# A linear-attention and gated-FFN kernel: lam moves to ScalarE's queue, and one activation table serves logarithm and exponential

## The chip, the cores and the metric

The kernel runs on one core of a Trainium2 chip. The metric is device time in microseconds (us) from one execution; lower is better. Three runs of the kernel before took 203.37, 203.39 and 203.57 us. The engines are TensorE (PE, with its weight loads PEld), VectorE (DVE), ScalarE (ACT), GpSimd (POOL) and SyncE (SP). SyncE computes nothing here; it issues transfers. GpSimd and ScalarE can issue transfers too, each on its own queue. The transfers of all queues run on the core's 16 DMA engines.

## The reference

Two parts follow each other. First a decayed linear attention over q, k and v of shape (4, 8, 768, 64), with one decay `lam` for each of 8 heads:

```
Dmask = where(rel >= 0, lam ** rel, 0)
for each block b of 64 positions:
    intra = ((qb @ kb.T) * Dmask) @ vb
    inter = (qb * lam ** (pos + 1)) @ kv_state
    out[b] = intra + inter
    kv_state = lam ** 64 * kv_state + (kb * lam ** (63 - pos)).T @ vb
```

Then, with x the attention output as 3072 tokens of 512 features:

```
h = x @ w_in        # 512 -> 2048
g = h * cos(h)
y = g @ w_out       # 2048 -> 512
```

## The kernel before

The 3072 tokens are 24 blocks of 128. The powers of lam are not computed by powers: a logarithm of lam is taken once (`lnl`), multiplied by positions (`expo_sp`, `expo`), and exponentials of that scale q, k and v ahead of the matmuls (`q_sp`, `k_sp`, `q_scale`, `v_scale`). These few small instructions on ScalarE and VectorE stand in lines 215 to 230. lam comes as a broadcast of 8 numbers to 128 partitions (4 KB, 32 bytes for each partition) by a transfer that SyncE issues in line 188. ScalarE reads its functions from tables. The build puts a table load ahead of an activation whose function isn't in the loaded set: one ahead of the logarithm (L216), one ahead of the first exponential (L221), and one ahead of a sine (L232), which is computed once on a dummy so that the table for the cosine of the FFN is there early.

The first four blocks are loaded as two "spans" of two blocks each, so that a transfer moves longer pieces: SyncE issues q, k of span 0 and then q, k of span 1 (called q0, k0, q1, k1 here; tile `sp_f`, L269, 512 KB each). GpSimd issues v of both spans (`v_sp`) and then the weights `w_in` and `w_out`, on its own queue; the first v load waits until q0 has landed. Each span load is scaled in two halves (L609): q0, k0 and q1 on VectorE, k1 on GpSimd, 1.29 us and 2.04 us for the pair of halves. TensorE transposes the halves (L617), ScalarE copies the transposes to SBUF (L620), TensorE multiplies scores (L628), VectorE masks them (L633), and TensorE makes the values (L641, L654, L660). From there on the hidden layer (L748, cosine on ScalarE L754, product on VectorE L760) and the projection (L794) fill TensorE, with the attention of later blocks worked in between.

The order on every engine is written by a planner: each piece of work is a task with an engine, a duration, what it depends on and a priority, and `Planner.order` simulates all engines and DMA and emits tasks in order of their planned start. `Planner.SETUP` gives the time at which each engine, and the DMA, is free for its first task. Where the plan leaves TensorE idle in the lead-in, `keep_awake` puts matmuls on a blank tile or on the identity into the gap (L882, L886), of a width that follows from the planned gap; their result is not used.

Of the kernel before, what the change touches and what calls it, by code (L numbers as in the profile page):

```python
# [56 lines left out]
class Planner:  # L57


    LAT = {"PE": 0.2, "ACT": 0.06, "DVE": 0.08, "POOL": 0.1, "SP": 0.0, "DMA": 0.0, "SETUP": 0.0}  # L60

    SETUP = {"POOL": 3.7, "DVE": 5.6, "ACT": 7.3, "SP": 1.3, "DMA": 2.9}

    def __init__(self, bufs):
        self.tasks, self.bufs = [], bufs
# [6 lines left out]
    def order(self):  # L72
        free, done = dict(self.SETUP), []
        got = {tag: [] for tag in self.bufs}
        owner = [None] * BANKS
        only = {}
        todo = list(self.tasks)
        while todo:
            first = {}
            for t in todo:  # L80
                if only.get(t.eng, t) is not t:
                    continue
                at = self.ready(t, got)
                if at is None:
                    continue
                if t.banks:
                    b = self.free_banks(t, owner)
                    if len(b) < t.banks:
                        continue
                    t.bank = b[:t.banks]  # L90
                    at = max([at] + [x for x, _ in t.bank])
                at = max(at, free.get(t.eng, 0.0))
                first.setdefault(t.eng, []).append((at, t))
            best = None
            for eng, c in first.items():
                t0 = min(a for a, _ in c)
                a, t = min(((a, t) for a, t in c if a <= t0 + 1e-6 + t.worth), key=lambda x: x[1].issue.end if eng == "DMA" else x[1].prio)
                if best is None or a < best[0]:
                    best = (a, t)
            assert best, "no task can start"  # L100
            a, t = best
            t.start, t.end = a, a + t.dur
            free[t.eng] = t.end
            only.pop(t.eng, None)
            if t.then:
                only[t.eng] = t.then
            if t.get:
                got[t.get].append(t)
            if t.banks:
                t.bank = [i for _, i in t.bank]  # L110
                for j, i in enumerate(t.bank):
                    owner[i] = (t, j)
            todo.remove(t)
            done.append(t)
        return sorted(done, key=lambda t: t.start)
# [29 lines left out]
def kernel(  # L145
# [10 lines left out]
    nc = tc.nc  # L156
    B, H, S, D = q.shape
    P = 128
# [26 lines left out]
        return psum.tile(shape, dt, tag=f"bank{i}", bufs=1, name=name)  # L185

    lam_bc = consts.tile([P, H], F32)
    nc.sync.dma_start(out=lam_bc, in_=bass.AP(tensor=lam.tensor, offset=lam.offset, ap=[[0, P], [1, H]]))
    pos = consts.tile([P, NB], F32)
    nc.gpsimd.iota(pos, pattern=[[P, NB]], base=-S // 2, channel_multiplier=1,  # L190
                   allow_small_or_imprecise_dtypes=True)
# [657 lines left out]

    idle = pl.add("SETUP", 0.0, [], None, -1e9, banks=1)  # L850
    for x in range(SPANS):
# [74 lines left out]
```

## Time and profile before

| | |
|---|---|
| median of three runs | 203.39 us |
| span of the profiled execution, first to last instruction | 201.6 us |
| TensorE busy | 193.4 us (96%) |
| ScalarE busy | 120.6 us (60%) |
| VectorE busy | 116.1 us (58%) |
| GpSimd busy | 64.5 us (32%) |

The times of the profile are counted from the first instruction. The profile gives one execution only, and its span leaves out what lies before the first and after the last instruction, 1.8 us against the median. "The chain that ended last" follows the last instruction back, at each step to what released it. An idle time is put down to whatever came last by the profile. "SPq" is SyncE's work of issuing a transfer, "issue" is time in which an engine waited for nothing that the profile shows. In the transfer views "q1" is the queue of SyncE, "q0" that of GpSimd, and "q10" that of ScalarE.

### The profile page before, as it was taken

How to read it: one execution, taken by the hardware profiler on the slowest of the kernel's cores; microseconds unless marked ns; L12 is line 12 of the kernel's file. 1: busy time of each engine (PE TensorE's matmuls, PEld its weight loads, DVE VectorE, ACT ScalarE, POOL GpSimd, SP SyncE). 2: the span in 40 equal slices, each digit the busy share in tenths (PEclk: the TensorE clock that was granted, in tenths of full speed). 3: DMA queues.
4: the chain of work that ended last, by engine and by line, in shares of the span. 5: the costliest groups of instructions: out<-in, count | busy, mean ns of one | idle time of the engine just before them, and what ended most of it. 6: DMA issues, size and time to landing. Idle time of an engine off the chain costs nothing.

```text
span 201.6 us, 5921 instructions
## 1 busy us (share of the span) xinstructions
PE 193.4 (96%) x2444; PEld 116.7 (58%) x2472; DVE 116.1 (58%) x229; ACT 120.6 (60%) x242; POOL 64.5 (32%) x85
## 2 busy tenths in 40 slices
PE   6899999999999999999999999999999999999994
PEld 2467544557757857767658676755445544444442
DVE  2779782267855958758458575834578454444001
ACT  5988870239738868566639666654877464345120
POOL 5694003076045172735455372525500000000000
PEclk9999999999999999999999999999999999999999
DMA  4999999999879999999999899969900010111112
GB/s 125 320 192 193 201 206 227 197 208 215 210 187 235 253 221 221 233 159 247 214 281 234 187 225 220 234 146 283 233 0 3 3 52 0 52 55 52 52 52 104
DMA packets 96762, 33.94 MB, mean 168 GB/s; under 512 B 84832, under 2 KB 93792, under 8 KB 96736
## 3 DMA queue, kind: packets, MB, share of 16 engines
q1 hardware_dynamic: 89232, 28.78, 62.5%
q0 software_dynamic: 7360, 4.72, 16.4%
q8 instruction: 19, 0.31, 0.7%
q10 hardware_dynamic: 144, 0.07, 0.1%
q14 instruction: 7, 0.06, 0.1%
HBM read 27.27 MB, written 6.29 MB: 166 GB/s over the span
## 4 chain that ended last, share of the span: by engine, by line
PE 92%; DMA 3%; issue 1%; SPq 1%; POOL 1%; ACT 0%; POOLq 0%; ACTq 0%
PE ps_h L748 42%; PE ps_f L794 41%; DMA sp_f<-in_k_dram 3%; PE ps_s L423 2%; PE ps_o L518 2%; PE ps_kv L435 1%; PE ps_o L486 1%; SPq L269 1%; PE ps_o L654 1%; PE ps_kv L641 1%; POOL k_sp L609 1%; PE ps_x L486 0%; PE ps_t L375 0%; PE ps_t L617 0%; PE ps_o L660 0%
## 5 line engine op out<-in xcount | busy, mean ns | idle before, releaser
L760 DVE TENSOR_TENSOR g<-ps_h,cos 128x256 bf16<-128x256 f32 (+1 forms) x149 | 73.0, 501 | 42.0 <-ACT cos L754 41.1
L754 ACT ACTIVATE cos<-ps_h,halfpi 128x256 f32<-128x256 f32 (+1 forms) x149 | 75.8, 536 | 29.3 <-PE ps_h L748 28.2
L748 PE MATMUL ps_h<-xT,w_in_sb 128*128 128x256 bf16 (+1 forms) x591 | 90.4, 303 | 0.4 <-issue 0.2
L794 PE MATMUL ps_f<-w_out_sb,g 128*128 128x512 bf16 (+2 forms) x377 | 87.6, 370 | 2.1 <-issue 1.4
L748 PEld LDWEIGHTS <-w_in_sb 128*128 128x128 bf16 x596 | 57.6, 98 | 29.9 <-DVE xT L526 0.4
L794 PEld LDWEIGHTS <-g 128*128 128x128 bf16 x400 | 37.6, 98 | 37.2
L345 POOL TENSOR_TENSOR qk<-q_f,q_scale 128x512 bf16<-128x512 f32 x19 | 19.6, 1044 | 35.0 <-DMA q_f<-in_q_dram 23.8
L808 ACT COPY o_sb<-ps_f 128x512 f32<-128x512 f32 (+1 forms) x24 | 13.7, 572 | 24.7 <-PE ps_f L794 23.4
L353 POOL TENSOR_TENSOR v_s<-v_f,v_scale 128x512 bf16<-128x512 f32 x19 | 19.7, 1042 | 11.5 <-DMA v_f<-in_v_dram 9.0
L428 DVE TENSOR_TENSOR s_m<-ps_s,mask 128x512 bf16<-128x512 f32 x20 | 13.0, 685 | 4.2 <-PE ps_s L423 3.7
L349 POOL CAST qk<-k_f 128x512 bf16<-128x512 f32 x18 | 11.0, 611 | 7.9 <-DMA k_f<-in_k_dram 7.9
L526 ACT CAST xT<-ps_o 128x512 bf16<-128x512 f32 x11 | 6.0, 588 | 9.0 <-PE ps_o L518 5.7
L441 DVE TENSOR_TENSOR sum<-sum,ps_kv 128x512 f32<-128x512 f32 x15 | 10.2, 682 | 0.6
L446 ACT CAST S<-sum 128x512 bf16<-128x512 f32 x15 | 9.2, 617 | 0.9 <-DVE sum L441 0.8
L269 POOL DMA_DIRECT2D w_out_sb<-in_moe_w_out_dram x4 | 3.0, 784 | 15.6 <-DMA q_f<-in_q_dram 15.6
L808 DVE COPY o_sb<-ps_f 128x384 f32<-128x384 f32 x1 | 0.6, 558 | 11.5 <-DMA out_dram<-o_sb 11.5
L886 PE MATMUL ps_idle<-blank 128*128 128x512 f32 (+2 forms) x8 | 5.0, 770 | 1.6 <-DVE blank L212 1.6
L486 PEld LDWEIGHTS <-v_s 64*64 64x64 bf16 x320 | 4.0, 107 | 4.2 <-issue 3.4
L503 DVE COPY spare<-ps_o 1x1 f32<-1x1 f32 x6 | 0.9, 156 | 8.4 <-PE ps_o L486 8.4
L633 DVE TENSOR_TENSOR s_m_sp<-ps_s,mask_sp 128x512 bf16<-128x512 f32 x8 | 5.1, 685 | 1.2 <-PE ps_s L628 1.2
L486 PE MATMUL ps_o<-s_m,v_s 64*64 64x64 bf16 x256 | 5.1, 196 | 0.0
L518 PE MATMUL ps_o<-qkT,S 64*64 64x64 bf16 x304 | 4.9, 195 | 0.0
(74 smaller groups left out, 90.9 us busy)
## 6 DMA issues: line engine op xcount, KB each, us to landing
q_f<-in_q_dram SPq DMA_DIRECT2D x20, 256.0 KB, 3.7
k_f<-in_k_dram SPq DMA_DIRECT2D x20, 256.0 KB, 4.3
v_f<-in_v_dram SPq DMA_DIRECT2D x20, 256.0 KB, 4.9
out_dram<-o_sb SPq DMA_DIRECT2D x19, 256.0 KB, 2.6
w_out_sb<-in_moe_w_out_dram POOLq DMA_DIRECT2D x4, 512.0 KB, 12.3
sp_f<-in_q_dram SPq DMA_DIRECT2D x2, 512.0 KB, 5.2
sp_f<-in_k_dram SPq DMA_DIRECT2D x2, 512.0 KB, 5.8
w_in_sb<-in_moe_w_in_dram POOLq DMA_DIRECT2D x2, 512.0 KB, 8.6
```

What stands on the lines that cost most here:

```text
L345: vec[e].tensor_mul(new_qk()[:, 0, :, s], live.pop(("q_f", 2 * pr + s)), q_scale[:, c, :].unsqueeze(2).to_broadcast([P, H, D]))
L349: (nc.scalar.copy if early else nc.gpsimd.tensor_copy)(new_qk()[:, 1, :, s], live.pop(("k_f", 2 * pr + s)))
L353: vec[e].tensor_mul(live["v_s", 2 * pr + s], live.pop(("v_f", 2 * pr + s)), v_scale[:, c, :].unsqueeze(2).to_broadcast([P, H, D]))
L428: nc.vector.tensor_mul(t, live["s", pr][s], mask.unsqueeze(1).to_broadcast([P, H, D]))
L441: nc.vector.tensor_add(new, live["sum", pr, 0] if half else live["sum", pr - 1, 1], live["kv", pr][half])
L446: nc.scalar.copy(new_S(pr, half), live["sum", pr, half])
L486: yield lambda h=h: nc.tensor.matmul(o[halves[h % 2], h // 2], lhsT=live["v_s", n0 + s][m, h, :], rhs=live["s_m", n0 + s][m, h, :], start= ...
L748: nc.tensor.matmul(t[:, :n], lhsT=w_in_sb[:, kd, f * P:(f + 1) * P], rhs=live["xT", i][:, kd, at], start=(kd == 0), stop=(kd == KD - 1))
L754: nc.scalar.activation(c[:, :n], live["h", i, f, at.start][:, :n], AF.Sin, bias=halfpi)
L760: return nc.vector.tensor_mul(live["g", i][:, f, at], live.pop(("h", i, f, at.start))[:, :n], live.pop(("c", i, f, at.start))[:, :n])
L794: nc.tensor.matmul(live["f", i, j, piece][:, :width], lhsT=live["g", i][:, f, j * P:(j + 1) * P], rhs=w_out_sb[:, f, part], start=(f == 0) ...
L808: (nc.scalar.copy if eng == "ACT" else nc.vector.tensor_copy)(o[:, :width], live["f", i, j, piece][:, :width])
```

## The change

lam's transfer is issued by ScalarE in place of SyncE, so that q0 is SyncE's first transfer. Right behind it ScalarE loads one table set that holds both the logarithm and the exponential, which leaves two table loads in the kernel: this one and the sine's. The planner's set-up times for VectorE, ScalarE, SyncE and the DMA are lowered. Line numbers behind the edit are one higher in the changed kernel.

```diff
-    SETUP = {"POOL": 3.7, "DVE": 5.6, "ACT": 7.3, "SP": 1.3, "DMA": 2.9}
+    SETUP = {"POOL": 3.7, "DVE": 4.95, "ACT": 6.0, "SP": 0.85, "DMA": 2.45}
...
     lam_bc = consts.tile([P, H], F32)
-    nc.sync.dma_start(out=lam_bc, in_=bass.AP(tensor=lam.tensor, offset=lam.offset, ap=[[0, P], [1, H]]))
+    nc.scalar.dma_start(out=lam_bc, in_=bass.AP(tensor=lam.tensor, offset=lam.offset, ap=[[0, P], [1, H]]))
+    nc.scalar.preload_act_table_set("natural_log_exp_and_others")
     pos = consts.tile([P, NB], F32)
```

The new set-up times leave the order of all planned work as it was, on every engine. Only the fillers on TensorE differ: the first run of `keep_awake` is 512 + 512 + 128 columns wide in place of 512 + 512 + 256, the filler on the identity behind the second half of k0's transposes is gone, and the one ahead of k1's transposes is 512 columns wide in place of 320.

## The prediction

> **What bounds the kernel now.** I read the chain that ended last first, by share and then its opening stretch in order of time, because the change touches only the first microseconds.
>
> ```profile
> PE 92%; DMA 3%; issue 1%; SPq 1%; POOL 1%; ACT 0%; POOLq 0%; ACTq 0%
> ...
> 0.81 0.40 SPq L188
> ...
> 1.26 0.42 SPq L269
> ...
> 1.73 0.58 SPq L269
> ...
> 2.35 1.49 SPq L269
> ...
> 3.89 6.28 DMA sp_f<-in_k_dram
> ...
> 10.34 1.05 POOL k_sp L609
> ...
> 11.44 0.40 PE ps_t L617 x4
> ```
>
> The columns are start, duration and what. TensorE bounds the kernel from 11.44 us on: 92% of the chain is its matmuls, and its pieces follow each other with gaps of 0.05 to 0.16 us to the end. Nothing in the diff touches that. Ahead of it lies a lead-in set by SyncE's queue: lam's issue at 0.81, then q0, k0, q1, k1 (the two span loads of q and of k), then k1's landing at 10.17 and its scaling on GpSimd. The kernel gets shorter by as much as k1 lands earlier, if what meets it at 11.44 is earlier too.
>
> Second, the timeline of the lead-in on the other engines, because the change also reorders ScalarE.
>
> ```profile
> 0.80 1.28 ACT L216 ACT_TABLE_LOAD   x1 [0.80 <-PEq L910]
> ...
> 3.70 0.21 ACT L216 ACTIVATE lnl<-lam_bc 128x8 f32<-128x8 f32 x1 [1.62 <-DMA lam_bc<-in_lam_dram]
> 3.93 1.28 ACT L221 ACT_TABLE_LOAD   x1
> 4.02 0.18 DVE L218 TENSOR_TENSOR expo_sp<-pos_sp,lnl 128x16 f32<-128x16 f32 x1 [1.98 <-ACT lnl L216]
> ...
> 5.22 0.22 ACT L221 ACTIVATE q_sp<-expo_sp 128x16 f32<-128x16 f32 x1
> ...
> 5.47 1.29 DVE L609 TENSOR_TENSOR q_sp<-sp_f,q_sp 128x512 bf16<-128x512 f32 x2 [1.03 <-ACT q_sp L221]
> 5.59 1.96 POOL L269 DMA_DIRECT2D v_sp<-in_v_dram  x2 [1.93 <-DMA sp_f<-in_q_dram]
> 5.81 1.28 ACT L232 ACT_TABLE_LOAD   x1
> ...
> 7.22 1.29 DVE L609 TENSOR_TENSOR k_sp<-sp_f,k_sp 128x512 bf16<-128x512 f32 x2 [0.46 <-DMA sp_f<-in_k_dram]
> ...
> 8.71 1.29 DVE L609 TENSOR_TENSOR q_sp<-sp_f,q_sp 128x512 bf16<-128x512 f32 x2 [0.20 <-DMA sp_f<-in_q_dram]
> ```
>
> The brackets give the idle time before and what ended it. VectorE's first scaling waits for the factors q_sp (5.44), but q0's landing is nearly as late: 5.26 by the transfer view, 4.0 us after its issue. The next two scalings wait for loads, k0 and q1, with VectorE idle before each. So the table load at 3.93 holds VectorE back by some 0.2 us, which the wait for k0 swallows, and the loads set the pace.
>
> Third, the DMA view of 1.6 to 3.6 us (rates in 40 slices of 0.05 us), and of 6.5 to 9.0 us.
>
> ```profile
> GB/s 0 0 0 0 3 3 3 4 4 3 3 4 3 4 14 95 65 1 2 34 34 63 52 64 31 42 42 33 86 75 145 75 94 156 227 246 256 276 328 317
> DMA packets 418, 0.14 MB, mean 72 GB/s; under 512 B 144, under 2 KB 418, under 8 KB 418
> ```
>
> ```profile
> q1 hardware_dynamic: 1714, 0.87, 114.8%
> ```
>
> From 1.8 to 2.3 us only lam's 32-byte pieces move (3 to 4 GB/s); the first burst of q0 comes at 2.35, 1.09 after q0's issue at 1.26, and the rate needs until about 3.5 to reach the 347 GB/s that the second window shows. In that second window every packet is of SyncE's queue, though v_sp was issued on GpSimd's at 5.59.
>
> **The change, step by step.** All sums are made against the profiled execution: span 201.6 us, which stands 1.8 below the median of 203.39; I keep the 1.8.
>
> 1. lam's issue leaves SyncE: 0.40 and the 0.05 gap behind it. q0 issues at 0.81 instead of 1.26, the other three follow. If data follow issues at the same distance, q0, k0, q1 and k1 land 0.45 earlier, k1 at 9.72. v_sp (issued when q0 lands) and all weight loads behind it on GpSimd's queue move with them: -0.45 on the path.
>
> 2. How far lam's pieces themselves hold up q0 is not separable here. Lower bound of the gain: 0, if the same pieces hold the same DMA engines from 1.8 until about 3.3 whichever queue brought them. Upper bound: the stream runs at full rate from 0.81 + 1.04 = 1.85 instead of about 3.3, that is -1.45. I take 0.45 because the rows show the first q0 burst 1.09 behind its own issue, as lam's first piece is 1.0 behind its own; that is nearest to a plain shift.
>
> 3. lam's issue goes to ScalarE, ahead of everything there. By SyncE's row it costs 0.40, by the last store's row on ScalarE's queue 0.37. The table load then runs from about 1.25 to 2.53, still before lam lands at 3.7 (ScalarE idled 1.62 there): cost 0, cover 1.1 us. Nothing else is queued behind it that could start earlier.
>
> 4. The table load at 3.93 goes (1.28). The factor q_sp then waits only for expo_sp: 4.20, so q_sp is ready by 4.5 and q0's landing (4.81) ends the wait. Of the 1.28 the path gets nothing beyond step 1; the load of q0 is late next. The last table load moves from 5.81 to about 4.85 and no longer holds the first transposed copy (7.22), which becomes 0.5 to 0.9 earlier; kT's copies, behind k0's landing, move by 0.45 only.
>    The row here says 1.28 and an ACTIVATE 0.01 after the load. The Trainium skill, ScalarE: Activation LUTs, What ACT_TABLE_LOAD costs, prices a switch at about 2.66 us, with a drain of 1.38 that this trace doesn't show; by it ScalarE would save 2.66. The sum is the same by both, because the load of q0 covers it.
>
> 5. TensorE's keep-awake matmuls follow the planner's shifted set-up times: the opening run loses 128 columns of 1280, one filler behind the k0 transposes goes, and the one ahead of k1's transposes grows from 320 to 512 columns. All real work keeps its order on every engine. The grown filler: 320 columns took 0.76 from 10.38; 192 more at four passes are 768 columns, 0.33 us at the rate of the projection's row in the chain (28 matmuls of 512 columns in 6.21 us, 2.3 columns per ns). It starts at 10.38 - 0.45 = 9.93 and ends at 11.02; k1's first half is ready from GpSimd at 11.39 - 0.45 = 10.94, and its transposes began 0.05 later. Cost 0 to 0.05; I take 0. If k1 gains more than 0.5, this filler is late next, though it too moves with q1.
>    The opening run took 4.25 for its 1280 columns at four passes (1.2 columns per ns, against the 2.3 above), so the shorter one ends near 5.4, and the first transposes come at about 5.77: a gap of 0.4, as now (5.80 to 6.22). The Trainium skill, TensorE: Matmul & The Clock Gate, Part 1, speaks against a shorter run: full speed comes after a busy window of 3.41 us whose phase is free. By that rule the run of 3.85 leaves 0.44 for the phase where 4.25 left 0.84. The sum without the rule is 0; by it a missed window costs up to another window at half speed, over a stretch that mostly waits for loads.
>
> 6. From 11.44 on TensorE's work is the same and its loads move with the stream: w_in and w_out are queued behind v_sp. 0.
>
> Sum: 203.39 - 0.45 = 202.94, span about 201.15.
>
> **Rivals.**
>
> *More is gained* (0.2): lam's pieces no longer stand ahead of q0 in its queue, and the slow ramp shrinks. For it: 144 packets under 512 B in the window and 3 to 4 GB/s until 2.3. Between 0.6 and the bound of 1.45; middle 0.9, 202.5. TensorE's and VectorE's lead-in would have to follow, so I doubt the whole.
>
> *Nothing* (0.15): the ramp belongs to the first accesses or to lam wherever it is issued, and k1 lands between 9.9 and 10.2. For it: the bursts at 2.35 are followed by 0.6 us at under 70 GB/s, which an earlier issue may not cure. 203.1 to 203.4.
>
> *Slower: lam is served late* (0.15). q0 and lam now start within 0.01 us on two queues. In 6.5 to 9.0 us the engines served one queue alone while another had work issued. If lam waits behind q0, k0 or more, the factors are late. From lam's landing to VectorE's scaling are 0.8 us (3.69 to 4.49 without the load). VectorE has three scalings of 1.29 ahead of the masking at 9.92, so it must start by 5.60 to keep step 1, and by 6.05 to lose nothing: lam may land at 4.8, or 5.25. Behind q0 alone (4.81) it costs nothing much; behind k0 too (7.13 - 0.45 = 6.68) VectorE starts at 7.5 and ends at 11.35, +1.4, 204.8; behind all four +4, 207. Against it: lam has only 4 KB and nothing ahead of it at 0.8 us, and the ScalarE queue's one store landed 1.6 us after its issue, not later than SyncE's.
>
> *Slower: the clock comes late* (0.05). If full speed came only after the stretch from 10 to 15 us, its 4.7 us of TensorE work would take up to as much again; likelier 0.3 to 1. From 203.5 up.
>
> **How the numbers follow.** The plain shift has 0.45, with a spread of 0.3 to 0.65 for steps 2 and 5; three quarters of it lie beyond 0.2% (0.41 us, about what a measurement of this kernel can tell from no change). Faster: 0.34 + 0.2 = 0.54, and 0.01 of the third case. Within 0.2%: 0.11 + 0.13 = 0.24. Slower: 0.15 + 0.05, and 0.01 of the third = 0.21. The likeliest case alone is 202.7 to 203.1. The range for 8 in 10 reaches into the larger gain, 202.2, and to the mild end of a late lam, 203.9; outside it lie half of the two slower cases and the end of the larger gain.
>
> **What would show it.** Step 1: q0's issue at 0.81, k1 landing at about 9.7, GpSimd's scaling at 9.9, first k1 transposes near 11.0. Step 2: the rate passes 300 GB/s at 3.0 for a plain shift, at 2.0 to 2.5 for the larger gain, at 3.5 for none. Step 4: two table loads instead of three, and the first VectorE scaling ended by q0's DMA. The late lam would show as VectorE or ScalarE waiting for lam beyond 4.8, the late clock as transposes of 0.40 us growing longer after 6 us. I am wrong if k1 lands earlier and TensorE's start at 11.44 doesn't move: then the filler, a mask or w_in would end that wait.

## The result, and the profile after

The changed kernel takes 204.62 us (median of 6 runs, 204.00 to 205.52) against 203.38 for the kernel before (6 runs, 203.17 to 203.57). The ratio is 1.0067, 95% interval 1.0052 to 1.0083: 0.67% slower. The forecast was 202.9 with a range of 202.2 to 203.9: the time was to fall by 0.45 us and rose by 1.24.

The profiled execution of the changed kernel took 204.37 us, with a span of 202.7, 1.1 longer than before. These are rows of its lead-in on the timeline, those of the transfers and of what waits for them; the rows between are left out (start, duration, engine, line, what, and in brackets the idle time before it and what ended that; "ACTq" is ScalarE's work of issuing a transfer):

```profile
0.80 0.43 ACTq L188 DMA_DIRECT2D lam_bc<-in_lam_dram  x1
0.81 0.46 SPq L270 DMA_DIRECT2D sp_f<-in_q_dram  x1
1.32 0.57 SPq L270 DMA_DIRECT2D sp_f<-in_k_dram  x1
1.93 2.56 SPq L270 DMA_DIRECT2D sp_f<-in_q_dram  x1
4.46 0.21 ACT L217 ACTIVATE lnl<-lam_bc 128x8 f32<-128x8 f32 x1 [1.92 <-DMA lam_bc<-in_lam_dram]
4.53 1.45 SPq L270 DMA_DIRECT2D sp_f<-in_k_dram  x1
...
6.02 1.29 DVE L610 TENSOR_TENSOR q_sp<-sp_f,q_sp 128x512 bf16<-128x512 f32 x2 [0.82 <-DMA sp_f<-in_q_dram]
7.56 1.29 DVE L610 TENSOR_TENSOR k_sp<-sp_f,k_sp 128x512 bf16<-128x512 f32 x2 [0.25 <-DMA sp_f<-in_k_dram]
9.02 1.29 DVE L610 TENSOR_TENSOR q_sp<-sp_f,q_sp 128x512 bf16<-128x512 f32 x2 [0.16 <-DMA sp_f<-in_q_dram]
10.65 2.04 POOL L610 TENSOR_TENSOR k_sp<-sp_f,k_sp 128x512 bf16<-128x512 f32 x2 [0.96 <-DMA sp_f<-in_k_dram]
11.75 0.40 PE L618 MATMUL ps_t<-ident,k_sp 128*128 128x128 bf16 x4
```

q0 is issued 0.45 earlier, as the diff says. But everything that waits for data is later: q0's scaling starts at 6.02 instead of 5.47, k1's at 10.65 instead of 10.34, and k1's transposes at 11.75 instead of 11.44. lam is later too (its logarithm at 4.46 instead of 3.70). All three VectorE scalings, and GpSimd's, wait for a load.

The DMA view of 1.6 to 3.6 us of the changed kernel (40 slices of 0.05 us) shows where q0 lost its lead:

```profile
GB/s 0 0 0 0 1 3 3 1 1 3 1 1 3 1 2 1 3 3 1 55 42 72 62 64 64 52 33 43 42 72 74 115 115 115 85 115 114 135 124 146
...
q1 hardware_dynamic: 166, 0.08, 17.4%
q10 hardware_dynamic: 110, 0.00, 2.5%
```

Until 2.5 us only lam's 32-byte pieces move, now on ScalarE's queue (q10). q0's first burst comes at 2.55, 1.75 after its issue, where it was 1.09 before. After that SyncE's queue (q1) stays under 150 GB/s until 3.8 us, with lam's pieces still on their way. At 3.6 us it has moved 0.08 MB, where the same window before moved 0.14. By the packets of the trace, lam's 128 pieces took from 1.82 to 3.33 before and from 1.84 to 4.10 after, and the rate passed 300 GB/s at 3.5 before and at 4.2 after. In both kernels full speed comes when the last piece of lam is through.

At k1's transposes the changed kernel is 0.31 us behind. The rest of the 1.1 comes later. TensorE's work stands 0.66 behind at 21 us and stays near that until 139, where it falls to 1.04 behind. The page's group of weight loads for `w_in`, first before and then after, and a row from TensorE's waits after, name the two places:

```profile
L748 PEld LDWEIGHTS <-w_in_sb 128*128 128x128 bf16 x596 | 57.6, 98 | 29.9 <-DVE xT L526 0.4
...
L749 PEld LDWEIGHTS <-w_in_sb 128*128 128x128 bf16 x596 | 57.3, 98 | 30.5 <-DMA w_in_sb<-in_moe_w_in_dram 0.7
```

```profile
PE ps_s L424 <- DMA qkT<-qk: 0.3, 1, 0.3
```

Before, the longest wait named for that group was for VectorE (0.4 us), and no matmul waited for a transposed copy `qkT`. These two places are those of one execution (204.37, when the six took 204.00 to 205.52); another can lose its time elsewhere. The chain that ended last, by share, now has 8% of DMA where it had 3%:

```profile
PE 88%; DMA 8%; ACT 1%; SPq 1%; DVE 0%; issue 0%; ACTq 0%; DVEq 0%
```

So the loads are late at the start, and nothing makes that good later: between 36 and 60 us the kernel before moves 4.91 MB, the changed one 4.76. The difference is about what a shift of 0.66 us makes at 205 GB/s, an estimated 0.14 MB.

### The profile page after: what moved, and what is told of

Read it like the earlier page. It is cut to its first block, busy times and chain, and to the rows that moved or that the text cites. A ratio compares the mean times of both kernels' runs of the same rounds, so it can differ in the third digit from the quotient of the medians.

```text
span 202.7 us, 5946 instructions
## 1 busy us (share of the span) xinstructions
PE 196.5 (97%) x2471; PEld 116.5 (57%) x2471; DVE 116.2 (57%) x229; ACT 119.7 (59%) x241; POOL 64.5 (32%) x85
## 4 chain that ended last, share of the span: by engine, by line
PE 88%; DMA 8%; ACT 1%; SPq 1%; DVE 0%; issue 0%; ACTq 0%; DVEq 0%
PE ps_h L749 40%; PE ps_f L795 38%; DMA v_f<-in_v_dram 3%; DMA sp_f<-in_k_dram 3%; DMA qkT<-qk 2%; PE ps_s L424 2%; PE ps_o L519 1%; PE ps_kv L436 1%; PE ps_o L487 1%; PE ps_t L618 1%; PE ps_s L629 1%; PE ps_o L655 1%; PE ps_kv L642 1%; PE ps_x L487 0%; PE ps_idle L887 0%; PE ps_t L376 0%
## 5 line engine op out<-in xcount | busy, mean ns | idle before, releaser
L749 PE MATMUL ps_h<-xT,w_in_sb 128*128 128x256 bf16 (+1 forms) x596 | 91.4, 303 | 0.0
L795 PE MATMUL ps_f<-w_out_sb,g 128*128 128x512 bf16 (+2 forms) x400 | 91.3, 371 | 0.0
L442 DVE TENSOR_TENSOR sum<-sum,ps_kv 128x512 f32<-128x512 f32 x15 | 10.2, 682 | 0.6
L887 PE MATMUL ps_idle<-blank 128*128 128x512 f32 (+1 forms) x8 | 5.3, 811 | 1.6 <-DVE blank L213 1.6
```

The source lines that it names most:

```text
L442: nc.vector.tensor_add(new, live["sum", pr, 0] if half else live["sum", pr - 1, 1], live["kv", pr][half])
L749: nc.tensor.matmul(t[:, :n], lhsT=w_in_sb[:, kd, f * P:(f + 1) * P], rhs=live["xT", i][:, kd, at], start=(kd == 0), stop=(kd == KD - 1))
L795: nc.tensor.matmul(live["f", i, j, piece][:, :width], lhsT=live["g", i][:, f, j * P:(j + 1) * P], rhs=w_out_sb[:, f, part], start=(f == 0) ...
```

## The experiments

The theory after the result was: lam's 128 pieces, which all read one 32-byte address, run on the same DMA engines as q0 whichever queue brings them; next to q0 they take longer, hold q0 up longer, and the whole load stream starts later. Rivals were: the new table set or the fillers; a second queue at the start by itself; lam's own late landing; a late clock. "Ratio" is always against runs of the kernel before on the same chip, with a 95% interval.

### The change taken apart

Only the table set (lam stays on SyncE):

```diff
     nc.sync.dma_start(out=lam_bc, ...)
+    nc.scalar.preload_act_table_set("natural_log_exp_and_others")
```

> The table set alone: lam stays SyncE's first transfer and the set-up times of before are kept; the one table load stands ahead of the logarithm. Theory (two queues that start together share the DMA engines badly): nothing of that happens here, lam lands at 3.7, q0's first burst is at 2.35, TensorE's k1 transposes start at 11.3 to 11.5, time 203.2 to 203.4. Rival (the table set itself is slower, or a longer wait of ScalarE is behind the loss): 203.8 or more.

Measured: 203.30 us, ratio 0.9989 (0.9975 to 1.0003). lam's pieces run to 3.49, and k1's transposes come at 11.32. Removing the 1.28 us load is worth nothing that can be told from zero.

Only lam's queue:

```diff
-    nc.sync.dma_start(out=lam_bc, ...)
+    nc.scalar.dma_start(out=lam_bc, ...)
```

> lam on ScalarE's queue alone: three table loads and the set-up times of before. Theory (two queues together): lam's pieces last until about 4.1 instead of 3.3, the rate passes 300 GB/s near 4.2, k1's transposes start at 11.7 or later, time 204.0 to 205.5, as in the changed kernel; a bit worse still, since the second table load then ends near 6.0 and q0's scaling waits for it. Rival (the fillers that follow the set-up times are behind the loss): 203.0 to 203.5.

Measured: 204.21 us, ratio 1.0037 (1.0021 to 1.0054). lam's pieces run from 1.83 to 4.08, 300 GB/s is passed at 4.2, and on the timeline of this kernel the end of the lead-in reads:

```profile
1.93 2.61 SPq L269 DMA_DIRECT2D sp_f<-in_q_dram  x1
...
10.71 2.04 POOL L609 TENSOR_TENSOR k_sp<-sp_f,k_sp 128x512 bf16<-128x512 f32 x2 [0.97 <-DMA sp_f<-in_k_dram]
11.81 0.40 PE L617 MATMUL ps_t<-ident,k_sp 128*128 128x128 bf16 x4 [0.24 <-POOL k_sp L609]
```

The one line reproduces the late lead-in in full, and more than half of the loss. In this execution (203.76, near the fastest of its twelve) TensorE stays 0.37 to 0.44 behind to the end: nothing is added in the middle. So the part of the loss that comes behind the lead-in is not the same in every execution.

Only the planner's set-up times, that is, only the fillers:

```diff
-    SETUP = {"POOL": 3.7, "DVE": 5.6, "ACT": 7.3, "SP": 1.3, "DMA": 2.9}
+    SETUP = {"POOL": 3.7, "DVE": 4.95, "ACT": 6.0, "SP": 0.85, "DMA": 2.45}
```

> The set-up times alone, so only TensorE's fillers change. Theory (two queues together): transfers as before; the grown filler of 1.08 us in front of k1's transposes begins at 10.38 and ends at 11.46, at most 0.1 later than GpSimd's half is ready: 203.3 to 203.5. Rival (the fillers, or a later full clock, cost the time): 204 or more, with transposes that take longer than 0.40 before 10 us.

Measured: 203.26 us, ratio 0.9997 (0.9981 to 1.0014). No difference. k1's transposes come at 11.36. In the three profiles with lam first on SyncE's queue (before and the two parts without lam's move) they thus come at 11.32 to 11.44, so a tenth of a microsecond between two profiles means nothing here; the 0.31 to 0.37 of the kernels with lam on ScalarE's queue lie outside of that.

### No transfer of lam, and lam behind q0

```diff
-    nc.scalar.dma_start(out=lam_bc, ...)
+    nc.vector.memset(lam_bc, 0.98)
```

> The changed kernel without lam's transfer: VectorE writes 0.98 into the tile, so the output is that of another lam. It gives the ceiling of any way to load lam. Theory (lam's small pieces hold the engines): q0's first burst near 1.85, over 300 GB/s by 2.3, k1 lands at 8.6 to 9.2, its transposes start near 10.3, time 202.2 to 202.6. Rival (the first accesses after the start are slow whoever makes them): the rate still climbs for over 1 us after q0's first piece, passes 300 GB/s at 3.0 or later, and the time is 202.8 to 203.2.

Measured: 202.64 us, ratio 0.9969 (0.9952 to 0.9986). q0's first packet comes at 1.92, 300 GB/s at 3.0, k1's transposes at 10.53, 0.91 earlier than before. So some 1.1 us of slow start belong to the first accesses themselves and stay; lam's pieces cost the rest. The 0.91 shrinks to 0.63 by 21 us, because `w_in` doesn't come as much earlier.

```diff
+    (q0's load, issued here, first on SyncE's queue)
-    nc.scalar.dma_start(out=lam_bc, ...)
+    nc.sync.dma_start(out=lam_bc, ...)
```

> The changed kernel with lam back on SyncE's queue, but as its second transfer, behind q0. Theory A (two queues that deal pieces to an engine at the same time are the harm): in one queue lam's pieces come after q0's and hold the engines no longer than before; lam lands at 4.6 to 5.2, k1 lands at 9.8 to 10.1, time 203.1 to 203.4. Theory B (lam's pieces are slow wherever they stand, and every later load waits for them): k1 lands at 10.1 or later, 203.4 to 204.

Measured: 204.64 us (203.96 to 206.65), ratio 1.0082 (1.0050 to 1.0114). q0 starts as if lam weren't there (1.93, 300 GB/s at 3.0), but lam's pieces run from 3.96 to 5.53, and the factors come so late that VectorE's first scaling starts at 6.64. While they run, the stream that was already at speed breaks down: in the DMA view of 3.5 to 6.0 us it moves over 300 GB/s until 4.0, 52 to 119 from 4.2 to 5.0, and over 300 again from 5.6. There is one queue alone here, and the first accesses are long past, so neither is needed for lam's pieces to hold the loads up. TensorE then stands idle, and its clock goes. Two windows of this kernel's profile (of the slowest of its seven runs, 206.65), 9.0 to 12.5 and 12.5 to 15.9 us (busy time and count of PE, PEld, DVE, ACT, POOL, then the granted clock, DMA share and GB/s):

```profile
9.00:12.50 3.50, 3.32 (x46) 2.33 (x46) 3.10 (x6) 2.20 (x5) 1.03 (x2) 0.51 1.66 211
12.50:15.90 3.40, 3.40 (x34) 1.79 (x37) 0.72 (x2) 1.36 (x4) 3.40 (x6) 0.50 1.45 182
```

Both of the prediction's slower rivals are seen here, the late lam and the late clock. They are not what slowed the changed kernel in its profiled execution: there lam's logarithm was done at 4.67, q0's scaling waited for q0, and the clock was full from 5.64.

### Other ways to bring lam

128 other addresses, into an unused tile (lam is 0.98):

```diff
-    nc.scalar.dma_start(out=lam_bc, ...)
+    nc.vector.memset(lam_bc, 0.98)
+    rows = consts.tile([P, H], F32)
+    nc.scalar.dma_start(out=rows, in_=k[3, 7, 0:P, 0:H])
```

> The changed kernel, but ScalarE's early transfer brings 128 pieces of 32 bytes from 128 different rows of k into an unused tile, and VectorE writes 0.98 where lam would be, so the output is that of another lam. Same number, size, queue and time of pieces; only the source address differs. Theory C (128 reads of one address are what is slow): the pieces are done by 2.6, the rate passes 300 GB/s near 3.0 as without lam, time 202.5 to 202.9. Theory D (small pieces on a second queue are slow whatever they read): the pieces last until about 4, 300 GB/s at 4 or later, 203.7 to 205.

Measured: 205.20 us (203.65 to 206.62), ratio 1.0085 (1.0053 to 1.0117). The start was as without lam (pieces done at 2.83, 300 GB/s at 3.0), and yet the time was no better than that of the changed kernel. This contradicted the theory, until later runs showed that the added tile was to blame. The same tile was in the next kernel, which keeps lam's one address:

```diff
-    nc.scalar.dma_start(out=rows, in_=k[3, 7, 0:P, 0:H])
+    nc.scalar.dma_start(out=rows, in_=bass.AP(tensor=lam.tensor, offset=lam.offset, ap=[[0, P], [1, H]]))
```

> The kernel after, with the same load of 128 repeated pieces on ScalarE's queue into a tile that nothing reads, and lam taken as 0.98 from a memset (the output is that of another lam). If the loss is the load stream's alone, held up by the pieces: first q0 piece 2.5, 300 GB/s at 4.2, k1 lands at 10.5, time 204.2 to 204.9 as after. If the loss is lam's own late landing (factors, VectorE's queue), the time is 203.4 or less.

Measured: 207.33 us, ratio 1.0205 (1.0163 to 1.0247). It has the same transfers as the changed kernel, and loses 2.7 us more. Neither theory expected that.

One piece of 32 bytes, spread over the partitions by a TensorE product with ones (the opening fillers are rearranged for it):

```diff
-    nc.scalar.dma_start(out=lam_bc, ... ap=[[0, P], [1, H]]))
+    nc.scalar.dma_start(out=lam_row, ... ap=[[0, 1], [1, H]]))
...
+    nc.tensor.matmul(lam_bc, lhsT=ones, rhs=lam_row, start=True, stop=True)
```

> The changed kernel, but ScalarE loads lam once, 32 bytes into one partition, and TensorE spreads it to 128 partitions by a matmul with a column of ones, placed after the first 512 columns of the opening filler run; the logarithm reads PSUM. All theories that blame lam's 128 pieces: lam lands by 3.0, the factors are ready by 4.5, the loads run as without lam, time 202.5 to 202.9, faster than both kernels. Rival (any transfer on a second queue beside q0 costs): 203.5 or more.

Measured: 203.14 us, but from 202.45 to 204.42, ratio 0.9992 (0.9975 to 1.0009). k1's transposes come at 10.81, 0.63 earlier than before, as the theory wants. The profiled execution, one of 204.42, gives it back in the middle, at 44 us, by a wait that the kernel before doesn't have (TensorE's waits):

```profile
PE ps_o L493 <- DVE v_s L360: 1.7, 1, 1.7
```

The v block behind that wait was issued at 34 us and landed at 43 to 44.

The same single piece, first on SyncE's queue:

```diff
-    nc.scalar.dma_start(out=lam_row, ...)
+    nc.sync.dma_start(out=lam_row, ...)
```

> lam is loaded as one 32-byte piece, first on SyncE's queue as before, and spread over the partitions by a TensorE product with ones; nothing is on a second queue; table set and fillers as after. If it is lam's 127 repeated pieces that lengthen the lead-in, k1 lands nearly as without lam, plus the 0.45 of SyncE's issue (9.26 + 0.45 = 9.7), first k1 transposes at 11.0, and the time is 202.7 to 203.1, in a narrow spread. If before's pieces were hidden by the slow first accesses anyway, k1 lands at 10.1 and the time is 203.3. If a second queue at the start is what widens the spread of the runs, the spread here is as narrow as that of the kernel before (under 0.6 apart from single runs).

Measured: 203.10 us (202.93 to 203.81), ratio 0.9992 (0.9982 to 1.0001): k1's transposes 0.55 earlier, TensorE 0.36 earlier from 29 us on in the profile, and a time that can't be told from before. And the same piece behind q0 on SyncE's queue:

> As the kernel with one piece first on SyncE's queue, but q0 is issued first and lam's one piece second. q0 starts as without lam (first piece 1.9, 300 GB/s at 3.0). lam's piece stands behind q0's pieces on one DMA engine and lands at 4.8 to 5.3, so the factors come at 5.6 to 6.1 and VectorE's first scaling at about 5.9. The theory that pieces and not the queue cost the time: k1 lands at 9.3 to 9.7, first k1 transposes 10.6 to 11.2, time 202.4 to 203.0. The theory that any lam behind q0 is late: VectorE's queue ends above 10.4 and transposes come at 11.4 or later, time 203.3 or more.

Measured: 204.42 us, ratio 1.0060 (1.0038 to 1.0083). The piece landed at about 4.6, VectorE's first scaling started at 5.96, and the transposes took 0.63 each in place of 0.40, so the clock was late here as well. Both ways of putting lam behind q0 made it too late.

lam's issue behind the table load, to let q0's first accesses go ahead:

```diff
-    nc.scalar.dma_start(out=lam_bc, ...)
     nc.scalar.preload_act_table_set("natural_log_exp_and_others")
+    nc.scalar.dma_start(out=lam_bc, ...)
```

> The changed kernel with ScalarE's two first instructions swapped: the table load first, lam's issue at about 2.1, behind q0's and k0's. Theory A (two queues at once): lam's pieces now meet a running stream and land late, at 5 or beyond; q0's scaling waits for them, 203.5 to 206. Theory C (one address): the same 128 reads hold the engines a little later, k1 lands as in the changed kernel, 203.8 to 204.8. If lam lands by 4.5 and k1 by 9.9, both are wrong and the tie at the start was the harm.

Measured: 204.45 us, ratio 1.0052 (1.0037 to 1.0066). It didn't do what it was made for. On the timeline the issue starts 0.03 after the start of the table load, not 1.28 after it:

```profile
0.80 1.28 ACT L188 ACT_TABLE_LOAD   x1 [0.80 <-PEq L911]
...
0.83 0.42 ACTq L189 DMA_DIRECT2D lam_bc<-in_lam_dram  x1
```

So it is the changed kernel once more, with lam's pieces from 1.86 to 4.24 and 300 GB/s at 4.3.

### A later stream by itself, and the tile that misled

```diff
+    lam_row = consts.tile([1, H], F32)
+    nc.sync.dma_start(out=lam_row, ... ap=[[0, 1], [1, H]]))
     nc.sync.dma_start(out=lam_bc, ...)
```

> The kernel before with one more transfer, a single 32-byte piece of lam, ahead of lam on SyncE's queue; nothing else differs. It moves the whole load stream about 0.45 later, as the change did by 0.31, but with no second queue. If a later stream is all that the change did, the first k1 transposes come at 11.8 to 11.9 and the time rises by 0.4 to 1.0 (203.8 to 204.4), the part above 0.45 coming from waits for w_in and for loads in the middle. If the middle has slack for it, +0.0 to +0.2.

Measured: 206.37 us, ratio 1.0162 (1.0121 to 1.0203): 3 us for an issue of 0.35. Packets told why. In this kernel and in both with the tile `rows`, the 512-byte packets of q0 to k1 take 32 ns (median, 4.5 to 9 us), in every other kernel up to here 27. All three add a 32-byte tile in front of the others. So the tile alone was tried, without a transfer:

```diff
+    moved = consts.tile([P, H], F32)
+    nc.gpsimd.memset(moved[0:1, 0:1], 0.0)
     lam_bc = consts.tile([P, H], F32)
```

> The kernel before with one unused tile of 32 bytes ahead of the others in SBUF, and no transfer more. If the place of the tiles is what lengthened the packets in the kernel with one more piece on SyncE's queue and in both kernels with a dummy load: packets of the spans at 32 ns, k1 lands at 10.7 to 11, and the time is 1 to 3 us above that of before. If not, 203.4.

Measured: 206.24 us, ratio 1.0136 (1.0108 to 1.0164). The DMA view of 6.5 to 9.0 us, first of the kernel before, then of this one:

```profile
DMA packets 1714, 0.87 MB, mean 347 GB/s; under 512 B 19, under 2 KB 1714, under 8 KB 1714
```

```profile
DMA packets 1443, 0.73 MB, mean 290 GB/s; under 512 B 26, under 2 KB 1443, under 8 KB 1443
```

Moving the destination tiles by 32 bytes takes 16% of the rate. The runs with the added tile can therefore not be held against kernels without it. Against each other the two with the tile `rows` differ in the source address alone, and they say what the theory says: with one address the pieces last until 4.24 in place of 2.83, k1's scaling starts at 11.99 in place of 10.63, and the ratio is 1.0205 in place of 1.0085. Three kernels without the added 32 bytes replace them. The delay, with a tile of 512 bytes:

```diff
+    lam_row = consts.tile([P, 4 * H * 4], F32)
+    nc.sync.dma_start(out=lam_row[0:1, 0:H], ... ap=[[0, 1], [1, H]]))
     nc.sync.dma_start(out=lam_bc, ...)
```

> The kernel before with one more single 32-byte piece ahead of lam on SyncE's queue, in a tile of 512 bytes in place of 32, so that the alignment of all tiles behind it is as before. It moves the stream by 0.40 with nothing on another queue. Packets of the spans at 27 ns; k1 lands at 10.5 to 10.6 and first k1 transposes come at 11.8. If a later stream by itself makes the loss: 203.8 to 204.4. If the middle has slack: 203.4 to 203.7.

Measured: 204.23 us (203.97 to 204.52), ratio 1.0041 (1.0027 to 1.0054). Nothing is on another queue. k1's scaling starts at 10.55 and its transposes at 11.65, 0.21 later than before, yet the time grows by 0.84. The profile (of the slowest of the nine runs, 204.52) shows the rest in the middle. TensorE's work is 0.22 late at 29 us and 0.79 late at 70. First its weight loads' waits, then the page's chain by share:

```profile
PEld L425 <- DMA qkT<-qk: 1.6, 3, 0.6
```

```profile
PE 72%; DMA 12%; SPq 11%; POOL 2%; issue 1%; ACT 0%; DVE 0%; POOLq 0%; ACTq 0%
```

TensorE was 92% of the chain before; here loads and their issue are 23%, most of it between 30 and 70 us. In this execution the stream of loads had no slack there, and what started late at the front came back larger.

lam's load as in the changed kernel, but unread, so that nothing waits for it:

```diff
-    nc.scalar.activation(lnl, lam_bc, AF.Ln)
+    nc.vector.memset(lnl, -0.0202)
```

> The kernel after with lam's load on ScalarE's queue as it is, into the same tile, but nothing reads it: the logarithm of lam is a constant from a memset (0.98 for all heads, so the output is that of another lam). No tile is added, so every tile stays at its place in SBUF; the earlier dummy load added a 32-byte tile, and the 512-byte packets of the spans then took 32 ns each in place of 27. If the loss is the load stream held up by lam's pieces: rate over 300 GB/s at 4.2, k1 lands at 10.5, time 204.0 to 204.8. If the loss is lam's own late landing, time 203.4 or less.

Measured: 204.33 us (203.92 to 204.63), ratio 1.0030 (1.0005 to 1.0054; 3 of the 22 runs of before took 204.41 to 205.04, which widens it). The lead-in of its timeline:

```profile
1.92 2.59 SPq L270 DMA_DIRECT2D sp_f<-in_q_dram  x1
...
6.05 1.29 DVE L610 TENSOR_TENSOR q_sp<-sp_f,q_sp 128x512 bf16<-128x512 f32 x2 [3.39 <-DMA sp_f<-in_q_dram]
...
10.68 2.04 POOL L610 TENSOR_TENSOR k_sp<-sp_f,k_sp 128x512 bf16<-128x512 f32 x2 [0.96 <-ACT kT_sp L621]
```

VectorE idles 3.39 with its factors ready, and q0 comes as late as in the changed kernel. lam's own landing costs nothing that can be told. (In this execution the clock was full only from 10.95, so the way in which the profiled time came about is not quite the changed kernel's.)

And the same kernel with the 128 pieces taken from distinct rows of k, on the same second queue:

```diff
-    nc.scalar.dma_start(out=lam_bc, in_=bass.AP(tensor=lam.tensor, offset=lam.offset, ap=[[0, P], [1, H]]))
+    nc.scalar.dma_start(out=lam_bc, in_=k[3, 7, 0:P, 0:H])
```

> As the kernel with the unread lam, but the 128 pieces of 32 bytes come from 128 distinct rows of k. Packets of the spans at 27 ns again. If it is the one address that costs the time: first q0 piece 1.9, 300 GB/s at 3.0, k1 lands at 9.3 to 9.5 and the time is as without lam's transfer, 202.5 to 203.1. If any second queue at the start costs it: 204 or more.

Measured: 202.77 us (202.44 to 203.52), ratio 0.9975 (0.9959 to 0.9991). Its DMA view of 1.6 to 3.6 us, to be read against the one of the changed kernel above:

```profile
GB/s 0 0 0 0 4 25 43 129 153 106 104 62 164 154 123 72 92 113 82 113 109 83 82 63 92 154 174 256 348 348 328 297 358 348 358 338 358 338 348 338
...
q1 hardware_dynamic: 642, 0.33, 60.7%
q10 hardware_dynamic: 144, 0.00, 3.8%
```

Against the kernel with the unread lam the count of pieces, their size, the queues and the moment are the same. From distinct addresses the pieces are through at 2.80 in place of 4.13, q0 moves from 1.93, and 0.33 MB are there at 3.6 us in place of 0.09. q0's scaling starts at 4.84 in place of 6.05, k0's at 6.33 in place of 7.54; a load ends the wait before each, so the late clock of the other execution has no part in them. This pair decides between the causes named: the one address holds the stream up, not a second queue as such and not the small size of the pieces.

| kernel | lam's (or the dummy's) pieces, us | 300 GB/s at | k1's transposes | time, ratio |
|---|---|---|---|---|
| before | 1.82 to 3.33 | 3.5 | 11.44 | 203.4 |
| changed | 1.84 to 4.10 | 4.2 | 11.75 | 1.0067 |
| lam's queue only | 1.83 to 4.08 | 4.2 | 11.81 | 1.0037 |
| unread lam | 1.84 to 4.13 | 4.1 | 12.51 (late clock) | 1.0030 |
| one piece more on SyncE, 512-byte tile | to 3.74 | 4.0 | 11.65 | 1.0041 |
| unread distinct rows | 1.83 to 2.80 | 3.0 | 10.58 | 0.9975 |
| no lam | none | 3.0 | 10.53 | 0.9969 |

In each kernel of the table with lam's one address the rate passes 300 GB/s within 0.3 us of the last piece; in those without it, at 3.0.

## Why the prediction was wrong, step by step

1. *q0 0.45 earlier, the stream with it.* The issue moved as said (0.81). That data follow their issue at the same distance was wrong: the distance grew from 1.09 to 1.75, q1's issue on SyncE took 2.56 in place of 1.49, and k1 landed some 0.3 later, not at 9.72.

2. *How far lam's pieces hold q0 up: between 0 and -1.45, taken as the plain shift.* **This is the step that failed.** Its lower bound assumed that the pieces would be through at 3.3 whichever queue brought them, so the change could not lose here. Beside q0 they took 2.26 us in place of 1.51, so the bound was too good by 0.3 at k1: the term of -0.45 measured +0.31 at k1's transposes. The choice inside the bounds was wrong too. It read the first burst of q0, 1.09 after its issue, as an ordinary start; the row to read was the stretch after it, under 70 GB/s until 3.0 and at most 156 until 3.3, which ends with lam's last piece. The larger gain that the step priced is real (0.86 to 0.91 at k1's transposes in the two kernels without lam's address), but it comes from removing the repeated address, and moving it to another queue leaves it there.

3. *lam's issue on ScalarE costs 0, lam lands at 3.7.* The cost was right, since the unread lam is no faster beyond the uncertainty. The landing was wrong by 0.76 (the logarithm starts at 4.46 in place of 3.70), within the deadline of 4.8 that the rival named.

4. *The removed table load gives the path nothing.* Right: two loads are left, q0's landing ends VectorE's wait, and the table set alone measures 0.9989 (0.9975 to 1.0003). The last table load came at 5.58, not at 4.85, because lam was late; the first transposed copy hardly moved (7.20 in place of 7.22).

5. *Fillers cost 0 to 0.05.* Right by the run with the set-up times alone, 0.9997 (0.9981 to 1.0014). In the changed kernel the wider filler ends at 11.75, when k1's first half is ready as well. The shorter opening run was put at 3.85 and took 4.21, as long as the longer one before (4.25): full clock came at 5.64 there against 5.27 before. The transposes wait for q0, so this cost nothing in the profiled execution. The rule of the Trainium skill, TensorE: Matmul & The Clock Gate, Part 1, on windows of 3.41 us with a free phase, fits what the runs show: with lam second on SyncE's queue the clock was full for 3.4 us from 5.64, and then half for 6.8. Its warning did not decide the profiled execution of the changed kernel.

6. *The rest 0.* Wrong, and second in weight. Of the profiled execution's 1.04 on TensorE, 0.31 came from the lead-in, 0.35 from `w_in` until 21 us, and 0.38 from a transposed copy at 139 us. A delay of 0.21 at k1's transposes by one issue more on SyncE's queue went with 0.84 in the time. But with lam's queue alone 0.37 stayed 0.4 in its profiled execution, so this part varies. The reverse holds less well: 0.86 to 0.91 won at the front was worth 0.6 to 0.7.

Of the rivals, "nothing" had the mechanism (the ramp belongs to lam wherever it is issued), but put k1 at 9.9 to 10.2 at worst; it had no room for a loss. "More is gained" mistook the queue for the cause. The late lam and the late clock, the only slower cases, exist, and were shown with lam behind q0, but neither is what the profiled execution of the changed kernel shows.

**Left open:** lam's queue alone loses 0.83 us, the whole change 1.24, and the two intervals meet at 1.0052 to 1.0054. The shorter opening run of fillers together with the later q0 leaves TensorE idle longer, and in two executions of kernels with both (unread lam, issue behind the table load) the clock was full only at 10.6 to 10.95; whether that makes the difference was not measured. Why the same pieces take longer beside q0 than ahead of it is not shown either; they moved at 1 to 3 GB/s in place of 3 to 4 even before q0's first packet at 2.55. That the one address holds the engines up was shown against rows of k that lie 256 bytes apart; distinct addresses closer together, or copies of lam, were not tried. Nor is it known why most kernels with a transfer on ScalarE's queue vary more from run to run than the kernel before; the middle of the kernel, where loads came late in several profiles, is where the profile with one piece lost its time.

## What to carry to other kernels

A broadcast load that reads one small address once for each partition was not a small transfer here: price it by when its last piece is through, and take the time until then as time in which the loads beside it move slowly, on whichever queue they are. Before counting on an earlier issue, check in the DMA view whether the data were waiting for the issue or for other packets. And where the loads are the tight resource later on, a few tenths lost at the front can grow, in some executions if not in all, so "the rest is unchanged" needs a row that shows slack.

## What the runs showed of the hardware that was not expected

- 128 reads of 32 bytes from one address took 1.51 us ahead of q0 on one queue (1.51 to 1.69 in four profiles), and 2.26 beside it on two (2.25 to 2.40 in five); from 128 distinct rows, beside q0, 0.97 us (1.83 to 2.80). With one address the other queue got under 150 GB/s until 3.8 us and at most 220 until the last piece. Behind q0, in a stream at over 300 GB/s, they took 1.57 and cut it to 52 to 119 GB/s.
- Without lam's address the rate still needed from q0's issue at 0.81 until 3.0 to pass 300 GB/s, 1.1 of that after its first packet.
- The place of tiles in SBUF sets the cost of a packet: 32 bytes further, 512-byte packets took 32 ns in place of 27, and the kernel 2.85 us more. The Trainium skill, DMA: Bandwidth & Descriptors, How a descriptor splits into AXI transactions, says that a descriptor that doesn't start at a multiple of 256 bytes is read in more transactions; here the written side was moved. It gives beats, by which 512 bytes starting 32 off would need an estimated 17 in place of 16, 6% more; the measured 19% is larger. Which start addresses the tiles had was not looked at.
- A transfer issued by ScalarE behind a table load in program order started 0.03 us after the load's start; the issue doesn't wait for the 1.28 us of the load.
- The clock came to full at 4.8 to 10.95 us in kernels with nearly the same TensorE work. In the one with the table set only it came at 7.57, with no loss.
